# A clustered-attention and two-layer MLP kernel: the second weight block is read later, through the first staging buffer

## The chip, the cores and the metric

The program runs on one core of one Trainium2 chip. The metric is the device time of one execution in microseconds (us), the median over a few runs.

## The reference, cut to what matters

Attention over 16 (batch, head) pairs of 768 tokens with head size 64, in which a query sees only the keys of its own cluster; the heads are joined into x (1536 tokens by 512), and x goes through two MLPs of the same shape.

```python
mask = q_assign[:, :, :, None] == k_assign[:, :, None, :]
scores = np.where(mask, scale * q @ k.T, -1e9)
attn = exp(scores - max) / sum                     # softmax over the keys
x = (attn @ v) as (B * S, H * D)                   # 1536 x 512
h = x @ w_in;  x = np.maximum(0.01 * h, h) @ w_out # 512 -> 2048 -> 512
h = x @ w_in2; r = np.maximum(h, 0.0); out = (r * r) @ w_out2
```

All is float32. To keep that accuracy each factor of a matmul is held as a high part and a low part (`xh` and `xl`, `wh` and `wl`, `gh` and `gl`), and three of the four products are summed.

## The kernel before, in words

**Attention.** Two heads make a pair; there are 8 pairs and 48 units (`NU`), six units to a pair. A unit is 256 queries against 768 keys. Its steps are named in `PLAN`: scores on PE (`S0`, `S1`), the row maximum on DVE (`R0`, `R1`, L373), exp on ACT (`X0`, `X1`, L383), row sums on ACT and their reciprocal on DVE (`RE` L394, `RC` L397, the tile `r_t[u]`), the scaling of the rows on POOL (`N0`, `N1`, L400), transposes on PE (`T`, L413), the split into a high part on ACT (`H`, L424) and a low part on DVE (`L`, L430), the product with v on PE (`V`, L448) and two folds into `xt` on ACT and DVE (L461, L470). The number behind a name says how many units late the step is taken, so several units are under way at a time. At the end of a pair, POOL splits `xt` into `xh` and `xl` (`xsplit`, L476 and L478).

**Weight blocks.** The two MLPs have 16 blocks of 128 hidden features each, 32 in all. A block comes as 1 MB of 64-bit numbers, and `decode_pieces(ci)` makes float32 high and low parts of it in six pieces: the transfer on SP's queue (`load`, L121), a scaling on ACT (`mag`, L128), three integer steps on DVE (`shift` L132, `low` L138, `sign` L145), and `split` (a cast on ACT, L156, that writes `wh`, and a subtraction on POOL, L157, that writes `wl`). The raw numbers and the tile `wt` that the pieces work on have one buffer each in a staging pool, so a block's transfer can't start before the block ahead of it in that pool is past `sign`, and its `mag` can't start before the other is past `split`. There are two staging pools, `stg[0]` (opened for the last pair) and, behind the attention, `stg[-1]`, which lies where attention tiles were.

**Who orders what.** SP's queue is in program order throughout. The other four engines are in program order up to unit 42 (`NU - 6`, L682). From there a planner orders them at compile time: it runs the program through a clock of its own and lets each engine take, among the instructions that it believes ready, the one that comes first in the program. On the chip each engine then works through its list strictly in that order.

**Early blocks.** The first `EARLY` = 2 blocks are decoded during the last pair: their 12 pieces are dealt out over the last pair's steps, two to a step, block 0 in the first three and block 1 in the last three (L700 to L704).

**MLP.** A block's work for 512 tokens is one unit `U` of the MLP: 12 matmuls into `h` (`g1`, L725), the nonlinearity and the split of its result on ACT and DVE (`act`, L738 to L746), and, two units later, 12 matmuls into `o` (`g2`, L767). The first group has two blocks and three token ranges, so the units 0, 2 and 4 use block 0 and the units 1, 3 and 5 block 1. Units 0 and 1 need only tokens of the first batch. Units 2 to 5 also need the last pair's rows, for 3 of their 12 matmuls (kk = 3). `h` has four banks, those of the scores; `o` has four, those of the transposes and of the product with v. Blocks 2 to 31 are made during the MLP by a table (`plan`, L799 to L817): blocks 2 and 3 over the units 0 to 5.

Of the kernel before, what the change touches and what calls it, by code (L numbers as in the profile page):

```python
# [8 lines left out]
F32 = mybir.dt.float32  # L9
F32R = mybir.dt.float32r  # L10
I32 = mybir.dt.int32
# [41 lines left out]
def attention_moe_moe_kernel(  # L53
# [14 lines left out]
    NT, DM = out.shape  # L68
# [3 lines left out]
    NU = NP * 2 * (KC // 2)  # L72
# [3 lines left out]
    NBLK = NT // N  # L76
    G = 4
    GROUPS = ([2, 2] + [G] * (NF // G - 1), [G] * (NF // G))
    EARLY = 2
    RING = 8  # L80
    WARM = (9,4,10)

# [29 lines left out]
    stg = []  # L112

    def decode_pieces(ci):

        m, f = divmod(ci, NF)
        st = {}

        def load():
            st["raw"] = stg[-1].tile([128, 2 * DM, 2], I32, tag="wraw", name="wraw")  # L120
            nc.sync.dma_start(  # L121
                out=st["raw"].rearrange("p a b -> p (a b)"), in_=(w1, w2)[m][f].bitcast(I32)
            )

        def mag():
            t = stg[-1].tile([128, 2 * DM], I32, tag="wt", name="wt")
            st["t"] = t
            nc.scalar.mul(out=t.bitcast(F32), in_=st["raw"][:, :, 1].bitcast(F32), mul=W_SHIFT)  # L128

        def shift():  # L130
            t = st["t"]
            nc.vector.tensor_scalar(  # L132
                out=t, in0=t, scalar1=3, scalar2=None, op0=ALU.logical_shift_left
            )

        def low():
            t = st["t"]
            nc.vector.scalar_tensor_tensor(  # L138
                out=t, in0=st["raw"][:, :, 0], scalar=29, in1=t,
                op0=ALU.logical_shift_right, op1=ALU.bitwise_or,  # L140
            )

        def sign():
            t = st["t"]
            nc.vector.scalar_tensor_tensor(  # L145
                out=t, in0=st["raw"][:, :, 1], scalar=-0x80000000, in1=t,
                op0=ALU.bitwise_and, op1=ALU.bitwise_or,
            )

        def split():  # L150
            t = st["t"].bitcast(F32)
            pool = next(q for q, n in ring if ci % RING < n)
            wh = pool.tile([128, 2 * DM], F32R, tag="wh", name="wh")
            wl = pool.tile([128, 2 * DM], F32R, tag="wl", name="wl")
            weights[m, f] = (wh, wl)
            nc.scalar.copy(out=wh, in_=t)  # L156
            nc.gpsimd.tensor_tensor(out=wl, in0=t, in1=wh.bitcast(F32), op=ALU.subtract)  # L157

        return [load, mag, shift, low, sign, split]

    def pool_copy(out, in_):
        nc.gpsimd.tensor_scalar(
            out=out, in0=in_, scalar1=1.0, scalar2=1.0, op0=ALU.mult, op1=ALU.mult
        )
# [175 lines left out]
    s_t, e_t, r_t, et_t, a_t, xt_t, n_t = {}, {}, {}, {}, {}, {}, {}  # L340
# [331 lines left out]
    }  # L672

    early = [f for i in range(EARLY) for f in decode_pieces(i)]
    for u in range(-1, NU + 5):
        if u == NU - UPP:
# [7 lines left out]
        for op in PLAN[FIRST[u] if p == 0 else u % UPP].split():  # L684
            if ":" in op:
                name, lag = op.split(":")
# [5 lines left out]
            else:  # L692
                name, ahead = op.split("@")
# [107 lines left out]
    for m in range(2):  # L801
        f = 0
        for g, size in enumerate(GROUPS[m]):
            for i in range(size):
                if ci >= EARLY:
                    pcs = decode_pieces(ci)
                    at = last + i * (began - last) // size
                    n = max((began - last) // size, 1)
                    for k, pc in enumerate(pcs):
                        plan.setdefault(at + k * n // len(pcs), []).append(pc)  # L810
                ci += 1
            last = began
            for b in range(NBLK):
                for i in range(size):
                    units.append((m, b, f + i, g, i == 0, i == size - 1))
            began = len(units)
            f += size  # L817
# [60 lines left out]
```

## Time and profile before

| what | us |
|---|---|
| median of 3 runs | 793.46 (792.37 to 793.86) |
| profiled execution | 790.98 |
| its span | 789.2 |
| PE busy | 771.2 |
| DVE busy | 538.0 |
| ACT busy | 412.7 |
| POOL busy | 292.0 |

The span is the time from the first to the last instruction in the profile. The profiled execution's own time is 1.78 us longer than its span and 2.48 us below the median of the runs. In the tables by stage, a column gives an engine's busy time in that stretch and, in brackets, the number of its instructions; what is missing to the length of the stretch is idle time. PEclk is the granted clock of TensorE as a share of full speed.

### The profile page before, as it was taken

What the parts mean: (1) busy time and instruction counts of PE and PEld (TensorE: products, weight loads), DVE (VectorE), ACT (ScalarE), POOL (GpSimd) and SP (SyncE); (2) the same over time, 40 slices, a digit from 0 to 9 for tenths busy, and PEclk for the clock granted to TensorE, in tenths of its full rate; (3) what the DMA queues carried; (4) which work ended last, traced back from release to release, by engine and by line L of the source; (5) the groups of instructions that cost most, each with busy time, mean ns of one, the idle gap of its engine ahead of it and who ended that gap; (6) DMA issues with size and microseconds to landing.
All of it is one profiled execution on the core that took longest, in us unless ns stands there. A gap on an engine that the chain in (4) does not pass through costs nothing.

```text
span 789.2 us, 11011 instructions
## 1 busy us (share of the span) xinstructions
PE 771.2 (98%) x4147; PEld 664.4 (84%) x4147; DVE 538.0 (68%) x772; ACT 412.7 (52%) x759; POOL 292.0 (37%) x257
## 2 busy tenths in 40 slices
PE   8999999999989999999999999999999999999998
PEld 8899999999977778888888888888888888888886
DVE  5899999999997378876665568387356547533333
ACT  6988988988996464443432344345344334222221
POOL 2989889888854322122220124352022012100000
PEclk9999999999999999999999999999999999999999
DMA  7584574564510323123221022013112103000102
GB/s 222 120 205 108 109 173 116 113 153 91 125 54 2 107 106 107 60 100 108 107 107 54 1 106 82 26 54 108 54 53 107 54 0 108 1 0 1 45 23 94
DMA packets 16005, 66.35 MB, mean 84 GB/s; under 512 B 2704, under 2 KB 2704, under 8 KB 10960
## 3 DMA queue, kind: packets, MB, share of 16 engines
q1 hardware_dynamic: 15952, 65.64, 28.7%
q8 instruction: 33, 0.54, 0.3%
q14 instruction: 20, 0.16, 0.1%
HBM read 44.60 MB, written 3.15 MB: 60 GB/s over the span
## 4 chain that ended last, share of the span: by engine, by line
PE 81%; DVE 11%; ACT 4%; DMA 1%; issue 1%; POOL 1%; SPq 0%; DVEq 0%; ACTq 0%
PE o L767 33%; PE h L725 33%; PE A L448 5%; PE T L413 5%; PE S L350 5%; DVE el L430 3%; DVE nm L373 3%; ACT e L383 2%; DVE xt L470 1%; ACT eh L424 1%; DVE ds L276 1%; PE ohT L305 1%; DVE m L275 1%; DMA rqk<-qk 1%; DVE wt L138 1%
## 5 line engine op out<-in xcount | busy, mean ns | idle before, releaser
L157 POOL TENSOR_TENSOR wl<-wt,wh 128x1024 fp32r<-128x1024 f32 x32 | 76.8, 2400 | 292.6 <-ACT wh L156 235.6
L725 PE MATMUL h<-xh,wh 128*128 128x512 f32 x384 | 150.6, 393 | 2.2 <-DVE g L739 2.2
L725 PE MATMUL h<-xh,wl 128*128 128x512 f32 x384 | 150.6, 392 | 0.0
L725 PE MATMUL h<-xl,wh 128*128 128x512 f32 x384 | 150.5, 392 | 0.0
L746 DVE TENSOR_TENSOR gl<-g,gh 128x512 fp32r<-128x512 f32 x96 | 95.4, 994 | 47.6 <-ACT gh L745 47.5
L430 DVE TENSOR_TENSOR el<-T,eh 128x512 fp32r<-128x512 f32 x144 | 94.8, 683 | 7.8 <-ACT eh L424 6.0
L745 ACT CAST gh<-g 128x512 fp32r<-128x512 f32 x96 | 59.6, 621 | 73.0 <-DVE g L742 42.7
L400 POOL TENSOR_SCALAR e<-e,r 128x768 f32<-128x768 f32 x96 | 88.0, 927 | 20.1 <-DVE r L397 14.7
L373 DVE TENSOR_REDUCE nm<-S 128x1 f32<-128x768 f32 x96 | 90.7, 946 | 4.6 <-PE S L254 2.2
L350 PE MATMUL S<-hb 128*128 128x384 f32 (+1 forms) x384 | 90.6, 350 | 3.0 <-ACT e L383 2.6
L383 ACT ACTIVATE e<-S,nm 128x768 f32<-128x768 f32 x96 | 87.0, 906 | 11.7 <-DVE nm L373 7.4
L742 DVE TENSOR_TENSOR g<-t 128x512 f32<-128x512 f32 x48 | 39.4, 822 | 72.8 <-ACT t L741 72.7
L725 PEld LDWEIGHTS h<-xh,wh 128*128 128x128 f32 x384 | 72.2, 188 | 18.5 <-DVE g L739 2.6
L741 ACT ACTIVATE t<-h 128x512 f32<-128x512 f32 x48 | 28.7, 598 | 112.0 <-PE h L725 111.9
L424 ACT CAST eh<-T 128x512 fp32r<-128x512 f32 x144 | 79.6, 585 | 12.9 <-PE T L413 12.3
L725 PEld LDWEIGHTS h<-xh,wl 128*128 128x128 f32 x384 | 72.2, 188 | 16.0
L725 PEld LDWEIGHTS h<-xl,wh 128*128 128x128 f32 x384 | 72.2, 188 | 15.9
L448 PE MATMUL A<-eh,vv 128*128 128x256 f32 x288 | 79.5, 306 | 3.5 <-DVE xt L470 3.5
L413 PE MATMUL T<-ident,e 128*128 128x128 f32 x576 | 81.0, 274 | 1.1 <-DVE el L430 1.0
L738 ACT ACTIVATE t<-h 128x512 f32<-128x512 f32 x48 | 28.6, 598 | 95.6 <-PE h L725 95.6
L767 PE MATMUL o<-gh,wl 128*128 128x512 f32 x192 | 75.3, 392 | 0.0
L767 PE MATMUL o<-gh,wh 128*128 128x512 f32 x192 | 74.5, 393 | 0.8 <-DVE xt L470 0.8
(105 smaller groups left out, 1454.0 us busy)
## 6 DMA issues: line engine op xcount, KB each, us to landing
wraw<-w SPq DMA_DIRECT2D x32, 1024.0 KB, 4.7
hb<-spl SPq DMA_DIRECT2D x14, 576.0 KB, 4.8
hb<-spl SPq DMA_DIRECT2D x42, 192.0 KB, 5.0
rqk<-qk SPq DMA_DIRECT2D x16, 384.0 KB, 4.5
rv<-v SPq DMA_DIRECT2D x8, 384.0 KB, 3.6
out<-ob SPq DMA_DIRECT2D x12, 256.0 KB, 2.1
twice<-qk SPq DMA_DIRECT2D x8, 192.0 KB, 6.4
hb<-st SPq DMA_DIRECT2D x28, 48.0 KB, 2.7
```

The lines of the kernel that those rows point to most:

```text
L157: nc.gpsimd.tensor_tensor(out=wl, in0=t, in1=wh.bitcast(F32), op=ALU.subtract)
L350: nc.tensor.matmul(out=s[:, c, 0:HALF], lhsT=hb[0:k, a, i * 128 : (i + 1) * 128], rhs=hb[0:k, b, c * HALF : (c + 1) * HALF], start=(a == 0 ...
L373: nc.vector.tensor_reduce(out=n, in_=s_t[t][:, :, 0:HALF], axis=AX.XY, op=ALU.max, negate=True)
L383: nc.scalar.activation(out=e.rearrange("p (a b) -> p a b", a=2), in_=s_t.pop(t)[:, :, 0:HALF], func=AF.Exp, bias=n_t.pop(t), scale=1.0, ac ...
L400: nc.gpsimd.tensor_scalar(out=e_t[t], in0=e_t[t], scalar1=r_t[t // 2][:, t % 2 : t % 2 + 1], scalar2=1.0, op0=ALU.mult, op1=ALU.mult,)
L413: nc.tensor.transpose(T[:, o : o + 128], e_t[2 * u + b][:, kc * 128 : (kc + 1) * 128], ident)
L424: nc.scalar.copy(out=eh[:, 2 * g : 2 * g + 2, :].rearrange("p a b -> p (a b)"), in_=T_t[u, g])
L430: nc.vector.tensor_tensor(out=el[:, 2 * g : 2 * g + 2, :].rearrange("p a b -> p (a b)"), in0=T_t.pop((u, g)), in1=eh[:, 2 * g : 2 * g + 2, ...
L448: nc.tensor.matmul(out=A, lhsT=w, rhs=m[:, kc, :], start=(kc == 0 and i == 0), stop=(kc == KC - 1 and i == 1),)
L725: nc.tensor.matmul(out=h, lhsT=w[:, ws], rhs=x[:, kk, c], start=(kk == 0 and i == 0), stop=(kk == HP - 1 and i == 2),)
L746: nc.vector.tensor_tensor(out=gl, in0=g, in1=gh.bitcast(F32), op=ALU.subtract)
L767: nc.tensor.matmul(out=outs[o], lhsT=l, rhs=r, start=(first and i == 0), stop=(last and i == 2),)
```

## The change: one early block, and a transfer that waits

`EARLY` goes from 2 to 1. The six pieces of block 0 are now dealt out one to a step over all six steps of the last pair. Block 1 goes to the MLP's table, which puts all its six pieces behind unit 0 of the MLP, ahead of those of block 2. It keeps the staging pool of the last pair (`own = 0`), while all blocks from 2 on use the later pool as they did. Ahead of its transfer POOL copies the tile `r_t[NU - 3]`, the row sums (by then their reciprocals) of attention unit 45, into two elements of each row of the raw buffer, which the transfer then overwrites: so the transfer has to wait for unit 45's reciprocal, for the copy, and for block 0's `sign`.

```diff
-    EARLY = 2
+    EARLY = 1
...
         m, f = divmod(ci, NF)
         st = {}
+        own = 0 if ci < 2 else -1
 
         def load():
-            st["raw"] = stg[-1].tile([128, 2 * DM, 2], I32, tag="wraw", name="wraw")
+            st["raw"] = stg[own].tile([128, 2 * DM, 2], I32, tag="wraw", name="wraw")
+            if ci == EARLY:
+                pool_copy(out=st["raw"][:, 0].bitcast(F32), in_=r_t[NU - 3])
             nc.sync.dma_start(
                 out=st["raw"].rearrange("p a b -> p (a b)"), in_=(w1, w2)[m][f].bitcast(I32)
             )
 
         def mag():
-            t = stg[-1].tile([128, 2 * DM], I32, tag="wt", name="wt")
+            t = stg[own].tile([128, 2 * DM], I32, tag="wt", name="wt")
```

## Rows read from the trace of the kernel before

**Rows 1.** The page, busy time and share of each engine.

```profile
PE 771.2 (98%) x4147; PEld 664.4 (84%) x4147; DVE 538.0 (68%) x772; ACT 412.7 (52%) x759; POOL 292.0 (37%) x257
```

**Rows 2.** Busy time by stage: PE, PEld, DVE, ACT, POOL, then clock and DMA.

```profile
205.00:215.00 10.00, 10.00 (x79) 9.82 (x78) 9.61 (x19) 9.68 (x24) 7.78 (x7) 1.00 0.42 126
215.00:228.00 13.00, 11.70 (x85) 10.69 (x84) 12.68 (x20) 12.34 (x25) 6.57 (x5) 1.00 0.21 75
228.00:240.00 12.00, 9.17 (x65) 8.09 (x64) 11.81 (x17) 9.99 (x20) 8.02 (x8) 1.00 0.02 8
240.00:265.00 25.00, 24.86 (x154) 21.67 (x153) 15.01 (x26) 13.56 (x28) 7.07 (x7) 1.00 0.13 44
265.00:282.00 17.00, 14.05 (x64) 11.00 (x64) 10.15 (x13) 9.70 (x16) 6.87 (x4) 1.00 0.23 79
282.00:400.00 118.00, 118.00 (x516) 96.68 (x515) 88.41 (x102) 52.24 (x74) 25.65 (x11) 1.00 0.27 96
```

**Rows 3.** PE's waits from 205 to 300 us: total, times, longest.

```profile
PE h L725 <- DVE g L739: 2.2, 1, 2.2
PE A L448 <- DVE xt L470: 1.4, 1, 1.4
...
PE o L767 <- DVE xt L470: 0.8, 1, 0.8
```

**Rows 4.** The chain that ended last, in order of time: start, us, what.

```profile
236.63 2.47 DVE wt L145
...
259.59 4.66 DMA wraw<-w
```

**Rows 5.** The tile wt's instructions by stage: DVE, ACT, POOL, clock, DMA.

```profile
215.00:228.00 13.00, 3.10 (x3) 2.22 (x2) 2.20 (x1) 1.00 0.21 75
228.00:240.00 12.00, 4.45 (x3) 2.02 (x2) 0.18 (x1) 1.00 0.02 8
```

**Rows 6.** DVE in order of time: start, us, line, operation, idle before.

```profile
222.97 1.20 DVE L145 SCALAR_TENSOR_TENSOR wt<-wraw,wt 128x1024 int32<-128x1024 int32 x1
...
236.55 2.55 DVE L145 SCALAR_TENSOR_TENSOR wt<-wraw,wt 128x1024 int32<-128x1024 int32 x1
239.03 0.15 DVE L397 RECIPROCAL r<-r 128x2 f32<-128x2 f32 x1
```

**Rows 7.** POOL in order of time.

```profile
236.20 1.82 POOL L478 TENSOR_TENSOR xl<-xt,xh 128x768 fp32r<-128x768 f32 x1
239.35 1.79 POOL L400 TENSOR_SCALAR e<-e,r 128x768 f32<-128x768 f32 x2 [1.33 <-DVE r L397]
241.10 2.38 POOL L157 TENSOR_TENSOR wl<-wt,wh 128x1024 fp32r<-128x1024 f32 x1
...
268.01 1.86 POOL L162 TENSOR_SCALAR xh<-xt 128x768 fp32r<-128x768 f32 x1 [18.03 <-DVE xt L470]
269.95 1.85 POOL L478 TENSOR_TENSOR xl<-xt,xh 128x768 fp32r<-128x768 f32 x1
```

**Rows 8.** ACT in order of time.

```profile
229.34 1.16 ACT L128 ACTIVATE wt<-wraw 128x1024 f32<-128x1024 f32 x1
...
274.19 1.13 ACT L128 ACTIVATE wt<-wraw 128x1024 f32<-128x1024 f32 x1 [1.14 <-POOL wl L157]
```

**Rows 9.** PE in order of time.

```profile
245.41 0.48 PE L725 MATMUL h<-xh,wh 128*128 128x512 f32 x1
...
259.59 0.39 PE L725 MATMUL h<-xl,wh 128*128 128x512 f32 x1
...
264.24 0.40 PE L725 MATMUL h<-xh,wh 128*128 128x512 f32 x1
```

**Rows 10.** PE from 245.3 to 266 us by line: L413, L448, L725 in turn.

```profile
245.30:266.00 20.70, 4.27 (x28) 1.00 0.15 52
...
245.30:266.00 20.70, 5.51 (x36) 1.00 0.15 52
...
245.30:266.00 20.70, 14.79 (x59) 1.00 0.15 52
```

**Rows 11.** SP's own waits: total us, times, longest.

```profile
SPq L121 <- DVE wt L145: 382.0, 30, 34.6
...
SPq L121 <- PE T L413: 35.0, 1, 35.0
```

**Rows 12.** DMA issues: count, size, median us from issue to landing.

```profile
wraw<-w SPq DMA_DIRECT2D x32, 1024.0 KB, 4.7
```

## The prediction, made before the changed kernel was built or run

> **What bounds the kernel now.** I read the page's shares first: PE is busy 98% of the span [rows 1], so a change can only give back some of its idle time, or add to it. The table by stage says where that lies near the edit [rows 2]. Up to 215 us attention runs with PE full and DVE at 9.61 of 10. In the last pair DVE is full (12.68 of 13, then 11.81 of 12) and PE has holes: 13.00 - 11.70 = 1.30 us, then 12.00 - 9.17 = 2.83, together 4.13. From 240 to 265 it is the other way: PE is full, DVE has 15.01 of 25. The MLP's start, 265 to 282, has 17.00 - 14.05 = 2.95 us of holes, and from 282 PE is full for 118 us. Beside the edit there are thus 4.13 + 2.95 = 7.1 us to be won, 0.9%. PE's clock is 1.00 in every row, its level of 2.4 GHz, with the holes and without; I cost nothing for it.
>
> The waits name the holes [rows 3]: in the first stretch PE waits for folds on DVE and what hangs on them, in the second for DVE's `g` (2.2) and the last fold (0.8). The chain in order of time runs through the decoding itself: block 1's `sign` holds 2.47 us of it, block 2's transfer 4.66 [rows 4]. What the decoding takes is in the rows of the tile `wt` [rows 5]: block 0 has 3.10 us of DVE, 2.22 of ACT and 2.38 of POOL (the subtraction's row in [rows 7] stands for both), block 1 4.45 of DVE. The extra 1.35 is one instruction: block 0's `sign` took 1.20 us, block 1's 2.55 [rows 6]. It began at 236.55 beside a POOL subtraction that ran from 236.20 to 238.02 [rows 7] and ended 1.08 us behind that one's end, so it stood still beside POOL.
>
> **Block 1's decoding leaves the full stretch.** Its 4.45 us of DVE, and ACT's and POOL's parts, go behind unit 45's reciprocal, which ends at 239.18 [rows 6], into the stretch where DVE has 10 us free. That can give PE back no more than the 4.13 it lacks, and at worst nothing, if the attention steps that PE waits for are late for another reason. I take all of the 2.83 that lie beside block 1, and 0.4 of the 1.30 beside block 0, whose 3.10 us remain but are spread over six steps: -3.2.
>
> **Block 0's low part comes later.** Its last piece goes to the last step, where block 1's is now. That `wl` is ready at 241.10 + 2.38 = 243.48 [rows 7]; the first matmul into `h` starts at 245.41 [rows 9], by the first term at 245.4 - 3.2 = 242.2. If the low part moved not at all against today's block 1, PE would wait 1.3 us for the high and low parts; if it moved with the rest, nothing. Between 0 and 1.3 I take +0.7, the middle.
>
> **Block 1 is late for PE, or not.** Behind the first `h` matmul PE has work that doesn't need block 1: unit 0's 12 matmuls and 9 each of units 2 and 4 (kk 0 to 2). From 259.59 to 264.24 there are 20 matmuls, 0.2325 us each [rows 9]; 30 make 7.0. The attention that is left takes, in 245.30 to 266.00, what 59 matmuls leave: 20.70 - 59 x 0.2325 = 7.0 us, for 28 transposes and 36 products [rows 10]. So from 242.2 PE is supplied to 242.2 + 14.0 = 256.2. Block 1: the reciprocal at 239.18 - 3.2 = 236.0, two scalings that POOL takes ahead (1.79 [rows 7]), the copy, which no row shows: between DVE's 0.15 for the same two columns [rows 6] and half the POOL row of two scalings, 0.90, for 768; I take 0.2, nearest the small one, POOL having no more to do. Then 4.7 for the transfer [rows 12] and 2.22 + 3.10 + 2.38 = 7.70 for the pieces, end to end: 236.0 + 1.8 + 0.2 + 4.7 + 7.7 = 250.4. With the waits that block 1 has now from `mag` (229.34 [rows 8]) to the end of `wl` (243.48), 14.1 in place of 7.7, it is 256.8, and with no relief for the reciprocal and the dear copy 239.2 + 1.8 + 0.9 + 4.7 + 14.1 = 260.7. I take the middle of the first two, 253.6, inside the supply of 256.2: 0, with 4.5 us (260.7 - 256.2) for the late end.
>
> The Trainium skill speaks against this term ("SBUF — State Buffer", section "SBUF: two separate sides"): DVE and POOL share a pair of ports, which a DVE instruction with two inputs in SBUF and a POOL instruction hold in turn, "for the whole instruction". The 2.55 us `sign` agrees. By it, block 1's `low` and `sign`, moved to where POOL scales rows, subtracts block 0 and splits `xt`, would each stand still up to the 1.85 of a split [rows 7], so block 1 would come at 253.6 + 3.7 = 257.3, 1.1 behind the supply, and the sum below would lose that 1.1.
>
> **The queues.** The copy is in no one's way on POOL: all attention steps precede it in the program, and behind it in the same queue stands block 1's own subtraction. If POOL took it too early, ahead of unit 45's reciprocal, the scalings behind it would wait, but they need the same reciprocal. On SP every later weight transfer is behind block 1's. Block 2's has waited for the transposes 35.0 us [rows 11], until 259.59 [rows 4]; block 1's is issued near 238, so it holds up nothing, and what ends that wait is still the transposes, 3 us earlier.
>
> **The holes at 265 to 282.** The 0.8 goes if the last fold comes earlier and PE still has units 1, 3 and 5 to run. The 2.2 comes from order: ACT waited for POOL's subtraction of block 2 before block 3's `mag` [rows 8], and DVE did integer steps in front of `g`. Such a misplaced wait can remain, go, or come a second time for block 1: between -2.95 and +2.2; I take -1.0, the fold and a little.
>
> **The sum** against the profiled execution of 790.98: -3.2 + 0.7 + 0 - 1.0 = -3.5, that is 787.5. The median of the runs stands 2.48 above the profiled execution; there it is 793.46 - 3.5 = 790.0.
>
> **The rivals.** *All holes go* (0.10): the planner has DVE free and fills well, 7.1 less a remnant of 0.9 beside block 0: 793.5 - 6.2 = 787.3. For it: the supply of 14 us. Against it: it still misjudges times, as the 2.2 shows.
>
> *The gain is handed back at once* (0.22): attention ends 3 us earlier, but PE has half its filling (30 matmuls in place of 60) and waits those 3 us for block 1 or for the split of `xt`, 1.86 + 1.85 us on POOL and perhaps behind block 1's subtraction of 2.38 [rows 7]. Net between -1.6 and +1.6: 793.5. Here belongs, too, that the change doesn't do what it says: block 0's `sign`, now dealt to the fifth step, may end later than the reciprocal, so the added wait decides nothing and only the moved pieces count.
>
> *PE's list is wrong* (0.23), the slower side: the planner puts unit 1's matmuls where they are now, straight behind unit 0's, since its clock thinks block 1 ready. PE is in order, so at 242.2 + 2.8 = 245.0 it would stand until 253.6 with the last transposes and products behind it: at most 8.6 us, less the 3.5. It is slower from a wait of 3.5 us on; a planner that is wrong by twice to thrice the 2.2 it misjudged elsewhere (4.4 to 6.6) gives about +2 on the mean: 793.5 + 2 = 795.5, at most 793.5 + 5.1 = 798.6. Against it: in the stretch from 240 to 265 PE today has only 25.00 - 24.86 = 0.14 us of holes, though the list is as fixed there.
>
> **How the numbers follow.** The forecast has 0.45, with its own range of 788.0 to 791.8. What a measurement here can tell from no change is 0.2%, 1.6 us. Faster by more: 0.45 + 0.10 = 0.55; within: 0.22; slower: 0.23. The range leaves out half of *all holes go* and a third of *PE's list is wrong*: 787.0 to 796.2.
>
> **What would show it.** Right: in the profile after, PE's holes from 215 to 240 are 1 us or so, unit 47's reciprocal comes some 3 us earlier, block 1's three DVE pieces begin behind 242, its transfer starts within 3 us of unit 45's reciprocal, and the first product into `o` starts earlier than now. Wrong: an `h` matmul that waits on `wl` or `wh` for over 2 us with transposes behind it (*PE's list*); PE idle for ACT's or DVE's `g` for longer than 2.2 (handed back); holes in the last pair that stay near 4, so that DVE's load wasn't their cause.

## The result, and the profile after

| | median us | executions | TensorE's mean clock |
|---|---|---|---|
| before | 793.66 | 4, 792.37 to 793.92 | (profiled 1.0) |
| changed | 784.66 | 4, 784.27 to 785.69 | 1.0 in each |

The ratio is 0.9896, 95% interval 0.9883 to 0.9908: 9.0 us faster. The forecast was 790.0 in a range of 787.0 to 796.2, so the direction was right and the time lies 2.3 us below the range. Between the two profiled executions the gain is smaller, 790.98 - 784.71 = 6.3 us; most of the rest is put down to the clock in the experiments below.

The table by stage of the changed kernel (columns as in [rows 2]):

```profile
215.00:228.00 13.00, 11.68 (x86) 10.68 (x84) 12.67 (x20) 12.13 (x25) 6.71 (x6) 1.00 0.00 0
228.00:240.00 12.00, 12.00 (x95) 11.84 (x95) 11.91 (x22) 11.38 (x27) 9.09 (x11) 1.00 0.15 52
240.00:265.00 25.00, 23.93 (x138) 20.39 (x137) 17.35 (x25) 13.12 (x24) 11.96 (x7) 1.00 0.27 103
265.00:282.00 17.00, 17.00 (x75) 13.80 (x74) 12.75 (x15) 12.45 (x21) 3.70 (x2) 1.00 0.19 64
```

Against [rows 2]: the 1.30 us of PE's holes beside block 0 are there still (1.32). The 2.83 beside block 1 are gone, though DVE is as full as it was: it does attention there now. From 240 to 265 a new 1.07 stands against 0.14. The 2.95 at the MLP's start are gone. That is 7.22 - 2.39 = 4.8 us. PE's waits from 205 to 300 us are three now (before: [rows 3]):

```profile
PE T L416 <- DVE el L433: 1.0, 1, 1.0
PE A L451 <- DVE xt L473: 0.9, 1, 0.9
PE A L451 <- DVE el L433: 0.3, 1, 0.3
```

Block 0's and block 1's decoding, the instructions of the tile `wt` by stage (DVE, ACT, POOL, as in [rows 5]):

```profile
215.00:228.00 13.00, 3.10 (x3) 2.22 (x2) 2.38 (x1) 1.00 0.00 0
228.00:240.00 12.00, 0.00 (x0) 0.00 (x0) 0.00 (x0) 1.00 0.15 52
240.00:250.00 10.00, 3.23 (x3) 2.19 (x2) 0.09 (x1) 1.00 0.12 48
```

Block 0 is where it was, to the instruction. Block 1 has gone from 228-240 to 240-250, and its DVE steps cost 3.23 there in place of 4.45. SP's own waits, the copy on POOL, and DVE around block 1's steps:

```profile
SPq L124 <- POOL wraw L165: 13.0, 1, 13.0
```

```profile
236.88 0.19 POOL L165 TENSOR_SCALAR wraw<-r 128x2 f32<-128x2 f32 x1
...
243.65 3.30 POOL L403 TENSOR_SCALAR e<-e,r 128x768 f32<-128x768 f32 x2 [2.88 <-DVE r L400]
249.91 2.65 POOL L160 TENSOR_TENSOR wl<-wt,wh 128x1024 fp32r<-128x1024 f32 x1 [2.95 <-ACT wh L159]
259.69 1.86 POOL L165 TENSOR_SCALAR xh<-xt 128x768 fp32r<-128x768 f32 x1 [7.13 <-DVE xt L473]
261.63 1.85 POOL L481 TENSOR_TENSOR xl<-xt,xh 128x768 fp32r<-128x768 f32 x1
```

```profile
234.75 0.14 DVE L400 RECIPROCAL r<-r 128x2 f32<-128x2 f32 x1
...
243.64 0.69 DVE L135 TENSOR_SCALAR wt<-wt 128x1024 int32<-128x1024 int32 x1 [0.45 <-ACT wt L131]
...
244.85 1.33 DVE L141 SCALAR_TENSOR_TENSOR wt<-wraw,wt 128x1024 int32<-128x1024 int32 x1
...
247.30 1.21 DVE L148 SCALAR_TENSOR_TENSOR wt<-wraw,wt 128x1024 int32<-128x1024 int32 x1
248.54 0.43 DVE L473 TENSOR_TENSOR xt<-A,xt 64x256 f32<-64x256 f32 x1
```

The transfer's wait is real: 13.0 us on the copy, which POOL takes in 0.19 behind unit 45's scalings. Two things follow. `sign` (247.30) stands in front of a fold (248.54), and a product on PE waits 0.9 us for that fold: this is most of the new 1.07. And the split of `xt` begins at 259.69 where it began at 268.01 [rows 7]: 8.3 us earlier, though the first matmul into `h` moves only from 245.41 [rows 9] to 241.42. The chain in order of time shows why (start, us, what):

```profile
250.73 0.44 PE T L416 x4
251.17 5.12 PE h L728 x22
256.28 1.42 PE A L451 x12
257.70 3.94 PE h L728 x17
261.65 2.79 PE o L770 x12
```

With block 1 late, 12 + 22 = 34 `h` matmuls stand on PE ahead of the attention's last 12 products; before, it is 58 of the 59 that start up to 266 us [rows 10]. The 24 fewer are 24 x 0.2325 = 5.6 us of PE's time (the spacing worked out in the prediction), and with the 2.8 us of holes gone from the last pair, less the 0.9 that are new, they make an estimated 7.5 of the 8.3. The chain has no decoding step of block 2 in it any more, where [rows 4] had its transfer.

### The profile page after: what moved, and what is told of

Same layout as the page of the kernel before. It is cut to its first block, busy times and chain, and to the rows that moved or that the text cites. A ratio compares the mean times of both kernels' runs of the same rounds, so it can differ in the third digit from the quotient of the medians.

```text
span 782.9 us, 11015 instructions
## 1 busy us (share of the span) xinstructions
PE 770.1 (98%) x4147; PEld 665.3 (85%) x4147; DVE 532.2 (68%) x772; ACT 410.8 (52%) x759; POOL 293.4 (37%) x258
## 4 chain that ended last, share of the span: by engine, by line
PE 82%; DVE 12%; ACT 4%; issue 1%; POOL 0%; DVEq 0%; ACTq 0%; POOLq 0%
PE o L770 34%; PE h L728 33%; PE A L451 5%; PE S L353 4%; DVE el L433 4%; PE T L416 4%; DVE nm L376 4%; ACT e L386 2%; DVE xt L473 1%; ACT eh L427 1%; DVE ds L279 1%; PE warm L202 1%; PE ohT L308 1%; DVE m L278 1%; PE S L257 1%
## 5 line engine op out<-in xcount | busy, mean ns | idle before, releaser
L749 DVE TENSOR_TENSOR gl<-g,gh 128x512 fp32r<-128x512 f32 x96 | 91.6, 954 | 44.1 <-ACT gh L748 44.0
L744 ACT ACTIVATE t<-h 128x512 f32<-128x512 f32 x48 | 28.7, 598 | 113.3 <-PE h L728 113.2
L770 PE MATMUL o<-gl,wh 128*128 128x512 f32 x192 | 75.3, 392 | 0.0
L770 PE MATMUL o<-wh,gl 128*128 128x512 f32 x192 | 75.3, 392 | 0.0
```

The source lines that it names most:

```text
L749: nc.vector.tensor_tensor(out=gl, in0=g, in1=gh.bitcast(F32), op=ALU.subtract)
L770: nc.tensor.matmul(out=outs[o], lhsT=l, rhs=r, start=(first and i == 0), stop=(last and i == 2),)
```

## The experiments

Two theories stood at first. One: block 1's steps on a full DVE make all the holes, those of the last pair and, by a late attention, those of the MLP's start. Two: what counts at the MLP's start is PE's list, that is, how many `h` matmuls stand ahead of the attention's last products and so when `xt` is split. Times are medians; ratios are to the kernel before on the same chip, with 95% intervals.

**The wait taken away.**

```diff
-            if ci == EARLY:
-                pool_copy(out=st["raw"][:, 0].bitcast(F32), in_=r_t[NU - 3])
```

> The changed kernel without the copy that block 1's transfer waits for; block 1's pieces stay behind unit 0 of the MLP in the program and keep the first staging buffer. If the wait is what acts (first theory), the time is that of the kernel before, 793.5 us, within 0.3%, with 4 us of PE holes from 215 to 240 us. If the moved place in the program acts, it is near 785 us. Its several times also show how far executions of the same order differ: the profiled execution of before was 791.0, the others 792.4 to 793.9.

792.72 us, ratio 0.9996 (0.9987 to 1.0005). The instructions stand in the same order as before on every engine: that `EARLY` is 1, the pieces dealt otherwise, and block 1 behind unit 0 in the program changes nothing, because the planner goes by what it believes ready. The wait is the whole change. This run is thus a second profile of the order of before, and its span is 791.9 where that of before was 789.2. Its table by stage, then single microseconds behind the wait for `g`:

```profile
265.00:270.00 5.00, 4.11 (x24) 3.32 (x23) 3.52 (x4) 1.50 (x2) 1.11 (x1) 1.00 0.00 0
...
275.00:282.00 7.00, 4.66 (x17) 3.35 (x16) 5.50 (x8) 5.45 (x9) 0.04 (x1) 0.86 0.08 9
282.00:290.00 8.00, 8.00 (x33) 6.44 (x32) 6.18 (x8) 4.82 (x9) 2.40 (x1) 0.91 0.30 123
```

```profile
278.00:279.00 1.00, 0.00 (x0) 0.00 (x0) 0.97 (x2) 0.00 (x0) 0.00 (x0) 1.00 0.00 0
279.00:280.00 1.00, 0.84 (x4) 0.71 (x5) 1.00 (x3) 0.86 (x2) 0.00 (x0) 1.00 0.00 0
280.00:281.00 1.00, 1.00 (x4) 0.80 (x3) 1.00 (x2) 1.00 (x3) 0.00 (x0) 0.53 0.00 0
281.00:282.00 1.00, 1.00 (x4) 0.71 (x4) 1.00 (x3) 1.00 (x2) 0.00 (x0) 0.50 0.53 66
282.00:283.00 1.00, 1.00 (x4) 0.81 (x3) 1.00 (x3) 0.52 (x2) 0.73 (x1) 0.50 0.38 131
283.00:284.00 1.00, 1.00 (x5) 0.82 (x4) 0.91 (x2) 0.44 (x2) 1.00 (x1) 0.76 1.08 459
```

PE waited 2.34 us for `g`, ran again, and then its clock stood at 0.50, the level of 1.2 GHz: four matmuls are counted in a microsecond there, in place of six at 285. What that costs is 0.47 + 0.50 + 0.50 + 0.24 = 1.7 us, and PE counts as busy through it. (The Trainium skill, "TensorE: Matmul & The Clock Gate", section "What's actually happening", gives two states of the clock, 1.2 and 2.4 GHz, and ties them to how busy PE has been; the 0.50 and 1.00 here agree.) The drop isn't in the profile of before, but of the 73 executions of before that ran beside the experiments 8 have a mean clock of 1.0, with a median of 791.3 us, and 64 one of 0.998 or less, with 793.1: 1.8 us.

**Block 1's DVE steps left out of the kernel before.**

```diff
+        if ci == 1:
+            nop = lambda: None
+            return [load, mag, nop, nop, nop, split]
```

> The kernel before with block 1's three DVE steps (shift, low, sign) left out, so its weights are wrong; transfer, scaling, cast and subtraction stay early. Theory one, DVE's load makes the holes: the 2.83 us of holes from 228 to 240 go and the MLP's start gains too, -5 to -9 us. Theory two, PE's list makes the gain (unit 1's matmuls no longer stand ahead of the last transposes): only the holes of the last pair shrink, the split of xt still comes late behind unit 1's matmuls, the 2.95 us at 265 to 282 stay: -2 to -4 us.

789.07 us, ratio 0.995 (0.9937 to 0.9962), clock 1.0 in four of five. By stage:

```profile
228.00:240.00 12.00, 11.22 (x84) 10.40 (x84) 10.61 (x18) 11.09 (x25) 9.93 (x8) 1.00 0.17 71
...
265.00:270.00 5.00, 4.13 (x20) 3.14 (x19) 3.54 (x4) 1.41 (x2) 2.45 (x2) 1.00 0.18 25
...
275.00:282.00 7.00, 4.82 (x21) 3.67 (x20) 6.84 (x10) 5.25 (x10) 1.34 (x1) 1.00 0.26 68
```

The steps made the last pair's holes: 2.83 becomes 0.78. The holes at the MLP's start stay, 0.87 + 2.18. That is what the second theory forecast for this run (-2 to -4 us; measured -3.9): DVE's load is one part, and the MLP's start is another that doesn't follow from it. Of the 3.9, 2.0 are the holes that went; the mean clock is 1.0 in four of five executions, though the profile has the wait of 2.2 us as before.

**The wait on other units**, four runs that differ in one figure: the reciprocal of unit 43, 44, 46 or 47 in place of 45.

```diff
-                pool_copy(out=st["raw"][:, 0].bitcast(F32), in_=r_t[NU - 3])
+                pool_copy(out=st["raw"][:, 0].bitcast(F32), in_=r_t[NU - 5])   # 43; NU - 4, - 2, - 1
```

> The changed kernel with the wait on unit 43's reciprocal (226 us) in place of 45's, so that block 1's DVE steps stand in DVE's list before the attention's last steps, though later than in the kernel before. Theory one: the steps are still in DVE's full stretch, so holes of over 1.5 us remain there and the time is 789 to 793 us. Theory two: block 1 is late enough for unit 1 to stand behind the transposes, 785 to 788.

> The changed kernel with the wait on unit 44's reciprocal, between the changed kernel (784.7) and the run that waited on 43's (792.6). The planner puts block 1's DVE steps ahead of the last few attention steps and 20 matmuls of units 0 to 2 ahead of the last transposes. First theory (DVE's stretch): most of the last pair's 2.8 us of holes are gone, 787 to 790 us. Second theory (PE's list ahead of the attention's tail decides): the split of xt is late again and the hole of over 2 us near 277 us is back with the clock drop behind it: 789 to 792 us.

> The changed kernel with the wait on unit 46's reciprocal in place of 45's (238.7 in place of 234.8 us in the changed kernel's trace), the step between it and the run that waited on unit 47's (792.7). First theory (DVE's full stretch costs, and past it PE must have work until block 1 comes): the last pair as full as in the changed kernel, block 1's low part near 256 in place of 252.6, about at the end of PE's other work: 785 to 788 us. If the gain came from how late block 1 is, with no limit, it would be 784 to 785.

> The changed kernel with the wait on the reciprocal of the last unit, 47, in place of 45's; in the changed kernel's trace that comes at 243.0 in place of 234.8, 8.3 us later. Theory one: the last pair is as full as in the changed kernel, but block 1 comes near 260 and PE, which already had 1.1 us of holes from 240 to 265, runs out: 787 to 790 us. Theory two: with even less ahead of the attention's tail it is no slower than the changed kernel, 784 to 785.

| wait on unit | median us | ratio (95%) | PE's holes 215-240 | 240-265 | 265-282 | lowest clock of a stretch |
|---|---|---|---|---|---|---|
| none | 792.72 | 0.9996 (0.9987 to 1.0005) | 3.85 | 0.47 | 3.23 | 0.86, from 275 |
| 43 | 792.57 | 0.9992 (0.9983 to 1.0001) | 2.89 | 1.25 | 3.19 | 0.84, from 275 |
| 44 | 789.38 | 0.9959 (0.9946 to 0.9971) | 1.32 | 0.83 | 2.77 | 0.76, from 275 |
| 45 (changed, again) | 785.29 | 0.9907 (0.9894 to 0.9921) | 1.33 | 1.03 | 0.00 | 1.00 |
| 46 | 789.57 | 0.9957 (0.9944 to 0.9970) | 1.29 | 3.03 | 0.00 | 0.66, from 250 |
| 47 | 792.67 | 0.9995 (0.9987 to 1.0004) | 1.31 | 1.82 | 3.44 | 0.81, from 270 |

The optimum is one unit wide: 44 and 46, on the same chip as the row of 45, give back 4.1 and 4.3 us. Too early (43), the steps are still in DVE's full stretch. With 44 that stretch is clean, and what is lost lies at the MLP's start. Too late, PE's holes come while block 1 is still being made (with 46 a single wait of 2.4 us, for a fold) or behind it (with 47 one of 3.4, for `g`), and the clock falls: with 46 it stood at 0.50 for 6.8 of the 10 us shown here (a mean of 0.66).

```profile
250.00:255.00 5.00, 3.94 (x21) 3.54 (x22) 3.83 (x6) 1.90 (x3) 0.41 (x1) 0.66 0.15 26
255.00:260.00 5.00, 5.00 (x18) 4.13 (x18) 1.37 (x2) 1.12 (x1) 1.96 (x1) 0.66 0.44 184
```

With 47 the wait for `g` comes from order: ACT stands for 3.76 us in front of block 2's `mag` (L131) until its transfer has landed, with the nonlinearity (L741) behind it, and DVE takes block 2's `low` (L141) ahead of `g` (L742):

```profile
268.60 1.12 ACT L131 ACTIVATE wt<-wraw 128x1024 f32<-128x1024 f32 x1 [3.76 <-DMA wraw<-w]
269.61 1.08 ACT L741 ACTIVATE t<-h 128x512 f32<-128x512 f32 x2
...
270.48 1.23 DVE L141 SCALAR_TENSOR_TENSOR wt<-wraw,wt 128x1024 int32<-128x1024 int32 x1
271.73 0.69 DVE L742 TENSOR_TENSOR g<-h,t 128x512 f32<-128x512 f32 x1
```

**PE's list without the relief**: the kernel before, with only block 1's last piece held until unit 47's reciprocal and put behind unit 0.

```diff
             weights[m, f] = (wh, wl)
+            if ci == EARLY - 1:
+                pool_copy(out=wh[:, 0:2], in_=r_t[NU - 1])
...
     early = [f for i in range(EARLY) for f in decode_pieces(i)]
+    late = early.pop()
+    early.append(lambda: None)
...
+            if U == 0:
+                late()
```

> The kernel before with only block 1's last piece (high and low part) moved behind unit 0 and held until unit 47's reciprocal; its transfer and its three DVE steps stay in the last pair. PE's list then has 12 matmuls in place of 19 ahead of the next transposes. First theory, DVE's stretch is the cause of all: the last pair keeps its 2.8 us of holes and the time is that of the kernel before, 792 to 794 us. Second theory, PE's list makes the larger part: the 2.95 us of holes at 265 to 282 us and the half clock behind them go, the last pair's holes stay, 788 to 790 us.

791.89 us, ratio 0.9992 (0.9983 to 1.0001). The last pair keeps its holes (4.19) and so does the MLP's start (2.30, with a wait of 2.3 and the clock at 0.76 behind it). The edit moved the end of `xt`'s split only from 271.80 to 270.97, so it did not make the list of the changed kernel and can't decide between the theories: inconclusive for the second, and it only agrees with the last pair's holes belonging to DVE's steps, which stayed in place.

**The changed kernel again.**

> The changed kernel once more, beside these runs on one chip, for its spread: 784 to 786 us in all executions, with TensorE's mean clock at 1.0 in each, where most executions of the kernel before (26 of 29) show 0.995 to 0.998. If the clock drop were chance and not tied to the hole of 2.2 us, some of these would show it too, and lie near 786.5.

785.29 us, ratio 0.9907 (0.9894 to 0.9921), mean clock 1.0 in three executions and 0.999 in one. Over both sets, eight executions lie between 784.27 and 785.69, against 791.04 to 794.13 for before beside the later four.

**What the 2.2 us wait is.** Block 3's three DVE steps left out of the kernel before, and, in another kernel, a second buffer for `wt`:

```diff
+        if ci == 3:
+            nop = lambda: None
+            return [load, mag, nop, nop, nop, split]
```

```diff
-            t = stg[-1].tile([128, 2 * DM], I32, tag="wt", name="wt")
+            t = stg[-1].tile([128, 2 * DM], I32, tag="wt", name="wt", bufs=1 if ci < 2 else 2)
```

> The kernel before with the three DVE steps of block 3 (the fourth block) left out, so its weights are wrong; all up to 275 us is as before. It asks what ends the 2.2 us hole near 277 us and what the clock drop behind it is worth. If DVE's steps of block 3 in front of the first g make it (1.2 of the 2.2 us), the hole shrinks to about 1 us, the mean clock is 1.0 in most executions, and the time is 790 to 791 us, of which 1.2 is the hole and 1.5 the clock. If the hole is only PE having run out of work until the split of xt is through, it stays at 2 us or more and the time is 792 to 793.5.

> The kernel before with two buffers in place of one for the decoding's tile wt from block 2 on, all computed. PE's list is that of before up to the 2.2 us hole, but block 3's scaling no longer waits on ACT for POOL's subtraction of block 2 with the nonlinearity of units 2 to 5 queued behind it. If that order on ACT makes the hole, it goes or shrinks below 1 us, the clock stays at 1.0 and the time is 788.5 to 790.5 us; the 4.1 us of the last pair stay. If the hole is PE having nothing left until the split of xt is through, it stays at 2 us: 792 to 793.5.

Without the steps: 792.99 us, ratio 0.9998 (0.9989 to 1.0008). The wait is 2.1 as it was, since the planner now puts block 3's cast of 1.05 us in front of the nonlinearity on ACT. With two buffers: 790.57 beside 793.35, ratio 0.9968 (0.9958 to 0.9979). ACT no longer waits for POOL there, the one wait of 2.2 breaks into two, and the mean clock is 0.999 or 1.0 in seven of eight executions:

```profile
PE o L767 <- DVE gl L746: 1.3, 1, 1.3
...
PE h L725 <- ACT wh L156: 0.7, 1, 0.7
```

So the gain of 2.8 is 0.9 us of holes (2.95 to 2.01) and, by the mean clocks, most of the 1.8. Which order gave it isn't shown, since the planner moved instructions on ACT, DVE and PE together. Of the 0.9, 0.77 is the hole at 265-270, and that one lay on DVE: before, `low` of block 2 stands in front of the last fold; with two buffers the fold comes first (L138 and L470, before; then L470, two buffers):

```profile
266.24 1.22 DVE L138 SCALAR_TENSOR_TENSOR wt<-wraw,wt 128x1024 int32<-128x1024 int32 x1
267.49 0.43 DVE L470 TENSOR_TENSOR xt<-A,xt 64x256 f32<-64x256 f32 x1
...
266.69 0.43 DVE L470 TENSOR_TENSOR xt<-A,xt 64x256 f32<-64x256 f32 x1 [5.62 <-ACT xt L461]
```

The 2.0 us at 275-282 stayed, now 0.7 behind block 2's cast and 1.3 for `gl`, which took 2.46 us in place of 0.68 beside POOL's subtraction of block 2 (275.86 to 278.25). In both runs the edit put another step in the way, so they don't settle whether order or a lack of work made the 2.2 us.

**The two edits on the changed kernel**: block 1's DVE steps left out, and the second buffer.

> The changed kernel with block 1's three DVE steps left out, so its weights are wrong. If the 1.07 us of PE holes from 240 to 250 us in the changed kernel (a product that waits for a fold on DVE behind block 1's sign) are the price of the steps in their new place, they go and the time is 783.5 to 784.5; the 1.3 us beside block 0 stay. If the holes have another cause, the time is that of the changed kernel, 784.7 to 785.5.

> The changed kernel with two buffers for the tile wt from block 2 on, all computed. PE has no hole from 250 to 300 us in the changed kernel, so the second buffer has nothing to remove: 784 to 785.5 us, equal to the changed kernel. A gain of over 1 us would say that ACT's waits cost PE something that its holes don't show; a loss, that the new order makes a hole.

Without the steps: 785.64 us, ratio 0.9907 (0.9889 to 0.9924). The 1.07 are gone, as said, but a wait of 1.5 us for `g` has come at 270-275, so the time is that of the changed kernel. The steps in their new place cost nothing on balance. The second buffer: 785.13, ratio 0.9901 (0.9888 to 0.9915), no gain, as expected. No version here beats the changed kernel.

**What the runs have in common.** Work that needs neither the split of `xt` nor a block past 1 is 60 matmuls into `h` (two whole units and 9 each of four) and 24 into `o`. How many of these 84 are left when the split ends, counted by line up to that time, goes with the waiting behind it in all runs but one. The column "ahead" counts the `h` matmuls that PE has in front of the attention's last 12 products:

| kernel | ahead | split ends | matmuls left | waiting from 270 to 282 us |
|---|---|---|---|---|
| before | 58 | 271.80 | 5 | 2.18 |
| before, without block 1's steps | 58 | 271.26 | 4 | 2.18 |
| before, two buffers | 58 | 270.29 | 8 | 2.01 |
| wait on 43 | 60 | 272.51 | 1 | 2.57 |
| wait on 44 | 51 | 267.70 | 6 | 2.77 |
| block 1's last piece late | 51 | 270.97 | 2 | 2.30 |
| changed, without block 1's steps | 51 | 267.26 | 7 | 1.50 |
| changed | 34 | 263.48 | 24 | 0.00 |
| wait on 46 | 12 | 267.26 | 29 | 0.00 |
| wait on 47 | 12 | 259.34 | 53 | 2.48 |

24 matmuls are 24 x 0.2325 = 5.6 us of PE's work, and ACT's and DVE's steps on units 2 to 5 lie beside it. The wait on 44 and the changed kernel without block 1's steps come nearest to a test of PE's list: their last pair is as clean as the changed kernel's (1.32 and 1.30 us of holes), they have 51 matmuls ahead in place of 34, and the wait is back. Both also have block 1 earlier, so the list isn't changed alone. The wait on 47 doesn't fit: it has the most left and waits 3.44 us from 269.04, for the order on ACT and DVE shown above, so matmuls in hand are not enough where those two are late.

## Why the prediction was right or wrong

By its own terms, forecast against the two profiled executions:

| step of the prediction | forecast | measured |
|---|---|---|
| block 1's decoding leaves the full stretch | -3.2 | -2.8 (4.13 to 1.32) |
| block 0's low part comes later | +0.7 | 0 |
| block 1 is late for PE, or not | 0 | 0 |
| not in the sum: a fold behind block 1's `sign` | | +0.9 (0.14 to 1.07) |
| the holes at 265 to 282 | -1.0 | -2.95 |
| PE's clock | 0 | 0 here, -1.6 in the medians |
| not in the sum: the rest | | -1.4 |
| sum | -3.5 | -6.3 |

**The mechanism of the first term was right and nearly its size.** The run without block 1's steps shows that DVE's load made the holes. All the signs named for it came: 1.32 us of holes from 215 to 240, unit 47's reciprocal 4.5 us earlier (247.56 to 243.04), DVE's steps from 243.6, the transfer 2.2 us behind the reciprocal's end, the first product into `o` 4.9 earlier.

**The step that failed is "The holes at 265 to 282".** It took -1.0, "the fold and a little", and left the 2.2 us for `g` in place, put down to misplaced steps on ACT and DVE that could come again. It measured -2.95: the 2.2 went. Whether misplaced steps made them stays open: with the DVE steps gone 2.1 us of waiting stayed, with the second buffer 2.0, each time with another step in the way. The prediction had both numbers that bear on it: 30 `h` matmuls of filling in place of 60, and units 1, 3 and 5 still to run. It counted the smaller filling only as a danger for the time before block 1 comes; that the attention's tail then comes sooner, and PE has those units in hand when the split ends, it did not work out. In its place the runs show 34 `h` matmuls ahead of the attention's last products in place of 58, the split 8.3 us earlier and 24 matmuls in hand at its end in place of 5; that this is the cause is argued from the table above and not shown by an edit of its own. What happened is the rival *all holes go*, at 787.3, which had 0.10. Put right alone, the term gives 790.0 - 1.95 = 788.0, still inside the range; the time leaves it only with the clock.

**The second failure is a sentence: "I cost nothing for it", of the clock.** The profiled execution of before was one of the few without the drop; 64 of 73 have a mean clock as low as those that show it. The changed kernel has no wait over 1.0 us from 205 to 300 and no drop, so the medians should move by an estimated 64/73 x 1.8 = 1.6 us more than the profiles: 6.3 + 1.6 = 7.9, beside the measured 9.0 and 7.5; the 1.1 up to 9.0 stays open. The 2.48 us between the profiled execution and the median stood in the prediction as an offset to be added on both sides; for the most part it was a cost that the change could take away. With it the corrected sum is 788.0 - 1.6 = 786.4, below the range, and with the -1.4 of the last row but one it is 785.0. With the clock *all holes go* would have given some 785.7.

**Block 0's low part** did not move at all: dealing pieces to later steps of the program is no delay where the planner orders by readiness, as the run without the wait shows for the whole edit.

**The Trainium skill's rule on the shared ports** ("SBUF — State Buffer", "SBUF: two separate sides") was weighed at +1.1. DVE's `low` and `sign` took 1.33 and 1.21 us in the new place and did not stand still; beside them POOL's two scalings took 3.30 in place of 1.79 [rows 7]. The pair of ports was held, but POOL waited, which the rule allows and the sum by it did not. Block 1's low part was ready at 252.6, within the 250.4 to 256.8 worked out.

**The rival *PE's list is wrong*** was priced on the danger that unit 1's matmuls stand where they were. They did not: the planner believed the wait and put all but four of block 1's matmuls behind the attention's last products (34 ahead, of which 30 need no block 1). The runs on 46 and 47 show how near a late block 1 is, at 789.6 and 792.7.

**Open:** the -1.4 of the last row but one is 0.4 of holes ahead of the stretch (7.0 to 6.6 up to 205 us) and 1.0 of PE's busy time (771.2 to 770.2); neither was traced to a cause. And no run changed PE's list alone.

## What to carry to other kernels

Under a planner that goes by readiness, moving a piece in the program did nothing here; a wait on a datum of the right age moved it, and its place is worth trying a step to either side (here over 4 us each way). When filler work is taken away from a full engine, work out not only when the filling runs out but also what then comes sooner, and how much work is in hand when that is through. Ahead of a forecast, ask why the profiled execution is faster than the median: here it was the one without a clock drop.

## What the runs showed of the hardware that was not expected

A single wait of PE of 2.1 to 3.4 us in a stretch that is otherwise full was followed by a fall of the granted clock to 0.50 in seven of the nine profiles that have one; in two with 2.2 us (before, and before without block 1's steps) it stayed at 1.00. No profile here whose longest such wait was 1.5 us or less has such a drop, but one unprofiled execution each of two of these kernels (the changed one without block 1's steps, and before with two buffers) has a mean clock of 0.997 or 0.998, as low as executions with a drop. In the second profile of before's order the fall came 0.9 us after PE had started again, lasted 3.4 us and cost 1.7.
